# Loading order of batches 1 and 2 in an eight-batch attention and MLP kernel: the rest of k and v ahead of the main part, v ahead of the memsets, batch 2's k right behind w_out

## The chip, the core and the metric

The kernel runs on one core of one Trainium2 chip. That core has a matrix engine (PE), a vector engine (DVE), an activation engine (ACT), a general engine (POOL) and a sync engine (SP), and sixteen DMA engines that move data between the main memory and the on-chip memory. The metric is the device time of one execution in microseconds. Before the change it was 302.56 us, the median of three runs (302.47 to 302.97).

## What is computed

Attention over pooled keys and values, for 8 batches of 8 heads, 576 rows and 64 columns, and then a two-layer MLP over the 4608 resulting rows. Cut to what matters:

```python
k_p = k.reshape(B, H, 72, 8, D).mean(axis=3)      # eight rows pooled into one: 72 keys
v_p = v.reshape(B, H, 72, 8, D).mean(axis=3)
attn = softmax(q @ k_p.T / sqrt(D))
x = (attn @ v_p), as 4608 rows of 512
h = x @ w_in                                      # 512 x 2048
out = gelu_tanh(h) @ w_out                        # 2048 x 512
```

The 4608 rows are treated in nine groups of 512 (g = 0 to 8). A batch has 576 rows, so group g needs rows of batches g - 1 and g alone.

## The kernel before

The program is a software pipeline. While PE does the MLP of group g, the attention of batch g + 1 (called `nb`) is woven between the matrix products, and the inputs of batch g + 2 are loaded. The order on each engine is the order of the program text (`manual_schedule`), so an instruction that has to wait holds up all that stands behind it on its engine.

The pooled sums of k and v are made on DVE by three halving additions. A batch has 8 x 72 = 576 pooled rows of k, and the on-chip memory has 128 partitions: 512 rows (four per partition) are the main part, and the 64 rows left over, together with 64 rows left over of v, are a fifth slot called the rest. One function loads both:

```python
    def load_k(b, engs):
        rows = k[b].rearrange("h (j l) d -> (h j) (l d)", l=8)
        main = rows[0:128 * KR].rearrange("(p r) c -> p r c", r=KR)      # KR = 4
        n = KR // len(engs)
        for i, eng in enumerate(engs):
            eng.dma_start(out=kts[b % 2][:, i * n:(i + 1) * n], in_=main[:, i * n:(i + 1) * n])   # L74
        engs[0].dma_start(out=kts[b % 2][64:128, KR], in_=rows[128 * KR:])                         # L75
        rows = v[b].rearrange("h (j l) d -> j h (l d)", l=8)
        engs[-1].dma_start(out=kts[b % 2][0:64, KR], in_=rows[64:])                                # L77
```

Batches 0 and 1 use it and transpose their pooled keys on PE. From batch 2 on, another loader (`load_k_dma`, L82 to L85, the same bytes in another layout) is used, and q and the pooled keys are transposed by DMA (`trans_q_dma`, L264, and `trans_k_dma`, L185). The first loads behind batch 0's are issued by POOL in this order:

```python
    def load_rest():
        load_w_in(0, 2)
        load_w_in(2, 3)
        load_w_in(3, 4)
        load_k(1, [nc.gpsimd])
        load_q(1)
        for i in range(4):
            nc.gpsimd.dma_start(out=w_out_b[...], in_=w_out_v[:, i])       # L129
```

The three additions over the slots `c` (all five unless told otherwise), the small copy of the rest of v into the operand `vp` of the attention product, and the additions over half of batch 1's v:

```python
    def k_steps(b, c=slice(0, KR + 1)):
        t = kts[b % 2]
        return [lambda: add(t[:, c, 0:256], t[:, c, 0:256], t[:, c, 256:512]),     # add: L157
                lambda: add(t[:, c, 0:128], t[:, c, 0:128], t[:, c, 128:256]),
                lambda: add(kps[b % 2][:, c], t[:, c, 0:64], t[:, c, 64:128])]

    def v_moves(b):                                                                # L190
        (nc.scalar if b == 1 else nc.sync).dma_start(out=vps[b % 2][64:Sp, :, 0], in_=kps[b % 2][0:64, KR])

    def v_half(b, i):            # two of the four heads of each partition half
        t = vts[b % 2][:, 2 * i:2 * i + 2]
        ... two additions over t, then two more that write into vps[b % 2]         # all L157
```

At the end of batch 0's attention DVE clears buffers, and the load of batch 1's v follows one of these memsets (the SP queue waits for the one-column memset of L503, which stands there to set the moment of the load):

```python
    for t in kps:
        nc.vector.memset(t[:, KR + 1], 0.0)
    nc.vector.memset(kTs[1][0], 0.0)             # L498
    nc.vector.memset(kTs[1][1], 0.0)             # L499
    nc.vector.memset(vps[0], 8.0)                # L500

    for i in range(2):
        nc.vector.memset(vts[1][:, 2 * i, 0:1], 0.0)      # L503
    load_v(1, [nc.sync], 2)                               # four DMAs, L93
    nc.vector.memset(vps[1], 8.0)                # L505
    nc.gpsimd.memset(kz, 0.0)                    # L506
```

The loads for a later batch, called for batch 2 after the first half of group 0. The `gate` copies make POOL wait until something else has landed:

```python
        def load_next():
            if nb >= KX:                                                   # KX = 2
                nc.gpsimd.tensor_copy(out=gate, in_=eT[64:65, H - 1, 1, 0:2])
            if nb < KX:
                load_q(g + 2)                                              # L99
                trans_q_dma(g + 2)                                         # L264, issued by SP
                nc.gpsimd.tensor_copy(out=gate, in_=qTs[g + 2][0:1, 1, TP - 1, 0:2])   # L523
            if g + 2 >= KX:
                load_k_dma(g + 2)
            else:
                load_k(g + 2, [nc.gpsimd])
            load_v(g + 2, [nc.gpsimd])
            if nb >= KX:
                load_q(g + 2)
```

Group g has two halves. In the first, PE makes sixteen tiles of h (L406, four products each), ACT puts each through the gelu (L412), and side work is put behind the gelu with number `fo`:

```python
            kk = k_steps(nb) if nb < KX else k_steps_dma(nb)
            tk = [lambda: trans_k(nb, 4)]
            ...
            kk.append(lambda: v_moves(nb))
            ...
            else:           # g == 0
                tq = [...trans_q(nb, ...)...]
                plan = {0: kk[:-1], 11: kk[-1:], 13: tk, 14: tq[:1], 15: tq[1:3]}
```

In the second half PE makes the output (L415, 64 products, counted by m) with the attention of batch nb woven in. For group 0:

```python
                at(4, v_half, 1, 0)
                at(18, v_half, 1, 1)
            pos = (6, 14, 21, 27, 34, 41, 48, 55, 61)
            for i in range(len(ORDER) + 1):
                at(pos[i], qk, nb, *ORDER[i], 2)              # scores, L276
                a = (nb, *ORDER[i - 1], 4 + 2 * ((i - 1) % 2))
                at(pos[i], av, *a)                            # product with vp, L296
                at(pos[i], expo, nb, *ORDER[i], 2)            # ACT, L283
                at(pos[i], norm, *a)                          # ACT, L338, L339, L341
                at(min(pos[i] + 9, ...), mult, *a)            # DVE, L349: empties the banks that av filled
```

`av` alternates between two pairs of PSUM banks, so each `av` needs the `mult` of the one two places earlier to be done. DVE also empties the output banks: L650 (half sums kept for later), L421 and L424.

Of the kernel before, what the change touches and what calls it, by code (L numbers as in the profile page):

```python
# [18 lines left out]
def kernel(  # L19
# [9 lines left out]
    nc = tc.nc  # L29
# [13 lines left out]
    KR = 4  # L43
# [23 lines left out]
    KX = 2  # L67

    def load_k(b, engs):
        rows = k[b].rearrange("h (j l) d -> (h j) (l d)", l=8)  # L70
        main = rows[0:128 * KR].rearrange("(p r) c -> p r c", r=KR)
        n = KR // len(engs)
        for i, eng in enumerate(engs):
            eng.dma_start(out=kts[b % 2][:, i * n:(i + 1) * n], in_=main[:, i * n:(i + 1) * n])  # L74
        engs[0].dma_start(out=kts[b % 2][64:128, KR], in_=rows[128 * KR:])  # L75
        rows = v[b].rearrange("h (j l) d -> j h (l d)", l=8)
        engs[-1].dma_start(out=kts[b % 2][0:64, KR], in_=rows[64:])  # L77

    def load_k_dma(b):
        rows = k[b].rearrange("h (j l) d -> j h (l d)", l=8)  # L80
        for i in range(2):
            nc.gpsimd.dma_start(out=kts[b % 2][64 * i:64 * i + 64, 0:KR], in_=rows[0:64, 4 * i:4 * i + 4])  # L82
        nc.gpsimd.dma_start(out=kts[b % 2][64:128, KR], in_=rows[64:])
        rows = v[b].rearrange("h (j l) d -> j h (l d)", l=8)
        nc.gpsimd.dma_start(out=kts[b % 2][0:64, KR], in_=rows[64:])  # L85

    def load_v(b, engs, parts=1):

        rows = v[b].rearrange("h (j l) d -> j h (l d)", l=8)
        n = 4 // parts  # L90
        for r in range(0, 4, n):
            for i in range(2):
                engs[i % len(engs)].dma_start(out=vts[b % 2][64 * i:64 * i + 64, r:r + n],  # L93
                                              in_=rows[0:64, 4 * i + r:4 * i + r + n])

    def load_q(b, i0=0, i1=2):
        if b not in qs:
            qs[b] = qp.tile([128, 2, T * D], BF16, name="qb")
        nc.gpsimd.dma_start(  # L99
            out=qs[b][:, i0:i1],  # L100
            in_=q[b].rearrange("(i h) (p t) d -> (h p) i (t d)", i=2, t=T)[:, i0:i1])
# [7 lines left out]


    load_k(0, [nc.sync, nc.scalar])
    load_v(0, [nc.sync, nc.scalar])
    load_q(0, 0, 1)
    load_q(0, 1, 2)
# [2 lines left out]
    def load_w_in(k0, k1):  # L117
        nc.gpsimd.dma_start(out=w_in_b[k0 // 2][:, k0 % 2:k0 % 2 + k1 - k0], in_=w_in_v[:, k0:k1])
# [3 lines left out]
    def load_rest():  # L122
        load_w_in(0, 2)
        load_w_in(2, 3)
        load_w_in(3, 4)
        load_k(1, [nc.gpsimd])
        load_q(1)
        for i in range(4):
            nc.gpsimd.dma_start(out=w_out_b[:, 4 * i:4 * i + 4, :].rearrange("p j d -> p (j d)"), in_=w_out_v[:, i])  # L129
# [4 lines left out]
    kTs = [[consts.tile([128, H, Sp], BF16, name=f"kT{i}{e}") for e in range(2)] for i in range(2)]  # L134
# [6 lines left out]
    vps = [consts.tile([Sp, H, 2, D], BF16, name=f"vp{i}") for i in range(2)]  # L141
# [14 lines left out]
    def add(o, a, b):  # L156
        nc.vector.tensor_tensor(out=o, in0=a, in1=b, op=ALU.add)  # L157

    def k_steps(b, c=slice(0, KR + 1)):


        t = kts[b % 2]
        return [lambda: add(t[:, c, 0:256], t[:, c, 0:256], t[:, c, 256:512]),
                lambda: add(t[:, c, 0:128], t[:, c, 0:128], t[:, c, 128:256]),
                lambda: add(kps[b % 2][:, c], t[:, c, 0:64], t[:, c, 64:128])]

    def k_steps_dma(b):
        t = kts[b % 2]
        k0, k1 = (kz[:, :, e, e * D:e * D + D] for e in range(2))

        def third(o, p0, c):
            p = slice(p0, p0 + 64)
            return lambda: add(o, t[p, c, 0:64], t[p, c, 64:128])

        return [lambda: add(t[:, :, 0:256], t[:, :, 0:256], t[:, :, 256:512]),
                lambda: add(t[:, :, 0:128], t[:, :, 0:128], t[:, :, 128:256]),
                third(k0[:, 0:4], 0, slice(0, KR)), third(k0[:, 4:H], 64, slice(0, KR)),
                third(k0[:, H], 64, KR), lambda: nc.vector.tensor_copy(out=k1, in_=k0),
                lambda: trans_k_dma(b), third(kps[b % 2][0:64, KR], 0, KR)]
# [3 lines left out]
    def trans_k_dma(b):  # L183
        kxs[b] = bp.tile([128, 2 * H + 2, 64], BF16, name="kx", bufs=1)
        nc.sync.dma_start_transpose(out=kxs[b], in_=kz.rearrange("p h e c -> p (h e c)"))  # L185

    def v_moves(b):


        (nc.scalar if b == 1 else nc.sync).dma_start(out=vps[b % 2][64:Sp, :, 0], in_=kps[b % 2][0:64, KR])  # L190
# [10 lines left out]
    def v_steps(b):  # L201
        t = vts[b % 2]
        w = (vps[b % 2] if b else vz)[:, :, 0]

        def main():
            for i in range(2):
                p = slice(64 * i, 64 * i + 64)
                add(w[0:64, 4 * i:4 * i + 4], t[p, :, 0:64], t[p, :, 64:128])

        return [lambda: add(t[:, :, 0:256], t[:, :, 0:256], t[:, :, 256:512]),  # L210
                lambda: add(t[:, :, 0:128], t[:, :, 0:128], t[:, :, 128:256]), main]
# [25 lines left out]
    def trans_k(b, bank):  # L237
        trans_k_mm(b, bank)
        for e in range(2):
            trans_k_copy(b, e, bank)  # L240
# [17 lines left out]
    def trans_q(b, i, t0, n, bank, eng):  # L258
        trans_q_mm(b, i, t0, n, bank)
        trans_q_copy(b, i, t0, n, bank, eng)  # L260

    def trans_q_dma(b):
        qTs[b] = bp.tile([128, 2, TP, 128], BF16, name="qT")
        nc.sync.dma_start_transpose(out=qTs[b].rearrange("p i t c -> p (i t) c"),  # L264
                                    in_=qs[b].rearrange("p i c -> p (i c)"))
# [185 lines left out]

    nc.gpsimd.tensor_copy(out=gate[0:1], in_=kps[0][0:1, 0, 0:2])
    load_rest()
    scores(0, 0, 2)
    scores(0, 1, 0)
# [39 lines left out]
    mult0(1, 2, 2)  # L495
    for t in kps:
        nc.vector.memset(t[:, KR + 1], 0.0)
    nc.vector.memset(kTs[1][0], 0.0)  # L498
    nc.vector.memset(kTs[1][1], 0.0)  # L499
    nc.vector.memset(vps[0], 8.0)  # L500

    for i in range(2):
        nc.vector.memset(vts[1][:, 2 * i, 0:1], 0.0)  # L503
    load_v(1, [nc.sync], 2)
    nc.vector.memset(vps[1], 8.0)  # L505
    nc.gpsimd.memset(kz, 0.0)  # L506

    for fo, ko in [(fo, ko) for fo in range(6) for ko in range(2)]:
# [3 lines left out]
    for g in range(NG):  # L512
        nb = g + 1 if g + 1 < B else None
        act_set(GELU_SET)

        def load_next():

            if nb >= KX:
                nc.gpsimd.tensor_copy(out=gate, in_=eT[64:65, H - 1, 1, 0:2])  # L519
            if nb < KX:  # L520
                load_q(g + 2)
                trans_q_dma(g + 2)
                nc.gpsimd.tensor_copy(out=gate, in_=qTs[g + 2][0:1, 1, TP - 1, 0:2])  # L523
            if g + 2 >= KX:
                load_k_dma(g + 2)
            else:
                load_k(g + 2, [nc.gpsimd])
            load_v(g + 2, [nc.gpsimd])
            if nb >= KX:
                load_q(g + 2)  # L530

        if 0 < g and nb is not None and nb < KX:
            load_next()
# [1 line left out]

        side = {fo: [] for fo in range(FO)}
        if nb is not None:
            kk = k_steps(nb) if nb < KX else k_steps_dma(nb)
            tk = [lambda: trans_k(nb, 4)]
            if nb > KX:  # L540
                kk.append(lambda: trans_q_dma(nb))
            kk.append(lambda: v_moves(nb))
            vv = v_steps(nb)
            if nb >= KX:
                plan = {0: kk, 7: vv[:1], 8: vv[1:]}
            elif g:
                plan = {2: kk[:1], 3: kk[1:], 7: vv[:1], 8: vv[1:], 9: tk}
            else:
                tq = [lambda a=a, i=i: trans_q(nb, *a, QB[i], nc.vector) for i, a in enumerate(QG)]
                plan = {0: kk[:-1], 11: kk[-1:], 13: tk, 14: tq[:1], 15: tq[1:3]}  # L550
            for fo, what in plan.items():
                side[fo] += what

# [30 lines left out]
        if g == 0:  # L584
            load_next()
# [9 lines left out]
        if nb is not None and nb >= KX:  # L595
# [17 lines left out]
            if g + 2 < B:  # L613
                at(3, load_next)
# [41 lines left out]
    for c0, c1, bank in ((0, 384, o_bank(g, 3)), (384, DM, 4)):  # L656
# [5 lines left out]
        b, col = divmod(N - 128, S)  # L662
        t = col % CH // 32
        rows = out[b * S:(b + 1) * S].rearrange("(p t e) d -> e p t d", t=TP, e=2)
# [31 lines left out]
```

## Time and profile before

| what | value |
|---|---|
| time, median of 3 | 302.56 us |
| span of the profiled execution | 300.4 us |
| DVE, ACT, POOL busy | 152.7, 216.9, 38.2 us |
| bytes moved by DMA | 43.11 MB, 144 GB/s on average |
| start of group 0's matrix products | 20.0 us |
| group 0, second half | 34.9 to 54.65 us |
| group 1 | 54.65 to 85.89 us |
| groups 2 and 3, each | 31.08 us |

The views of the trace used here are the page of the whole run, the timeline of one engine (start, duration, line, operation, and in brackets how long the engine stood idle before and which event ended that), the table by stretches of time, the list of waits, and the chain of waits, which follows the work that ended last back to what released it. A line such as L157 is a line of the kernel before. A name such as `vp<-kp` says that `vp` is written from `kp`. In a line of POOLq, SPq or ACTq the duration is that of issuing a DMA and not that of the transfer. The trace also lists every DMA packet with its queue, size and start.

### The profile page before, as it was taken

How to read it: one execution, taken by the hardware profiler on the slowest of the kernel's cores; microseconds unless marked ns; L12 is line 12 of the kernel's file. 1: busy time of each engine (PE TensorE's matmuls, PEld its weight loads, DVE VectorE, ACT ScalarE, POOL GpSimd, SP SyncE). 2: the span in 40 equal slices, each digit the busy share in tenths (PEclk: the TensorE clock that was granted, in tenths of full speed). 3: DMA queues.
4: the chain of work that ended last, by engine and by line, in shares of the span. 5: the costliest groups of instructions: out<-in, count | busy, mean ns of one | idle time of the engine just before them, and what ended most of it. 6: DMA issues, size and time to landing. Idle time of an engine off the chain costs nothing.

```text
span 300.4 us, 4381 instructions
## 1 busy us (share of the span) xinstructions
PE 292.6 (97%) x1525; PEld 150.9 (50%) x1525; DVE 152.7 (51%) x308; ACT 216.9 (72%) x408; POOL 38.2 (13%) x69
## 2 busy tenths in 40 slices
PE   8799989999999999999999999999999999999995
PEld 3565545554555455545554555455545555445443
DVE  4785776475576257815690659155924630111112
ACT  1697677879888898789878988798879887206500
POOL 2614001300600060005000410033000000000000
PEclk9999999999999999999999999999999999999999
DMA  7999986871898169835994399729961210121022
GB/s 223 260 239 275 247 185 130 234 196 21 181 266 172 37 160 254 178 69 122 249 201 88 90 254 211 106 49 245 245 119 38 69 41 0 36 71 36 0 62 80
DMA packets 38806, 43.11 MB, mean 144 GB/s; under 512 B 25536, under 2 KB 26176, under 8 KB 38656
## 3 DMA queue, kind: packets, MB, share of 16 engines
q0 software_dynamic: 8016, 24.39, 35.7%
q1 hardware_dynamic: 30064, 17.06, 25.1%
q10 hardware_dynamic: 704, 1.38, 1.3%
q8 instruction: 12, 0.20, 0.3%
q14 instruction: 10, 0.08, 0.1%
HBM read 36.70 MB, written 9.44 MB: 154 GB/s over the span
## 4 chain that ended last, share of the span: by engine, by line
PE 78%; DMA 12%; DVE 4%; ACT 3%; issue 1%; SPq 1%; POOL 0%; DVEq 0%; POOLq 0%
PE PS L415 36%; PE PS L406 32%; DMA vt<-in_v_dram 5%; PE PS L331 4%; DMA kt<-in_v_dram 3%; PE PS L320 2%; DMA kt<-in_k_dram 2%; DMA qT<-qb 2%; DVE kt L157 1%; DMA kx<-kz 1%; PE PS L658 1%; ACT e L283 1%; PE PS L305 1%; ACT rc L365 1%; PE PS L276 1%
## 5 line engine op out<-in xcount | busy, mean ns | idle before, releaser
L415 PE MATMUL PS<-w_out_b,gT 128*128 128x512 bf16 x560 | 136.9, 379 | 0.0
L406 PE MATMUL PS<-xT,w_in_b 128*128 128x512 bf16 x576 | 126.2, 379 | 0.0
L412 ACT ACTIVATE gT<-PS 128x512 bf16<-128x512 f32 x144 | 79.3, 608 | 44.2 <-PE PS L406 44.1
L406 PEld LDWEIGHTS <-w_in_b 128*128 128x128 bf16 x576 | 65.1, 113 | 58.7
L415 PEld LDWEIGHTS <-gT 128*128 128x128 bf16 x560 | 53.9, 97 | 51.5 <-issue 2.1
L349 DVE TENSOR_TENSOR xT<-PS,rc 64x288 bf16<-64x288 f32 x112 | 51.0, 455 | 19.8 <-ACT rc L341 17.2
L421 DVE COPY osb<-PS 128x512 f32<-128x512 f32 x33 | 22.8, 692 | 50.0 <-PE PS L415 44.4
L326 ACT ACTIVATE eT<-PS 64x576 bf16<-64x576 f32 x48 | 30.7, 640 | 0.6
L313 DVE COPY eT<-er 8x576 bf16<-8x576 bf16 x24 | 7.3, 303 | 38.9 <-ACT er L311 38.3
L338 ACT ACTIVATE ld<-PS 64x288 f32<-64x288 f32 x56 | 22.6, 403 | 5.6 <-PE PS L331 5.1
L341 ACT ACTIVATE rc<-ld 128x288 f32<-128x288 f32 x56 | 24.9, 444 | 1.8
L157 DVE TENSOR_TENSOR kt<-kt 128x1280 f32<-128x1280 f32 (+5 forms) x18 | 18.9, 1048 | 11.5 <-DMA kt<-in_v_dram 7.5
L383 ACT ACT_TABLE_LOAD x17 | 21.8, 1283 | 3.6 <-issue 3.3
L339 ACT ACTIVATE ld<-PS 64x288 f32<-64x288 f32 x56 | 22.6, 403 | 1.4
L331 PE MATMUL PS<-eT,vp 72*128 72x288 bf16 x96 | 19.7, 285 | 0.0
L519 POOL COPY gate<-eT 1x2 bf16<-1x2 bf16 x5 | 0.9, 177 | 125.0 <-DMA eT<-er 125.0
L157 DVE TENSOR_TENSOR vt<-vt 128x512 f32<-128x512 f32 (+2 forms) x18 | 15.6, 865 | 1.4 <-DMA vt<-in_v_dram 1.0
L331 PEld LDWEIGHTS <-vp 72*128 72x128 bf16 x96 | 9.5, 98 | 11.3
L283 ACT ACTIVATE e<-PS 72x576 bf16<-72x576 f32 x16 | 9.9, 644 | 4.5 <-PE PS L276 4.4
L435 PE MATMUL PS<-idle 128*128 128x512 bf16 x31 | 8.9, 433 | 1.2 <-DVE idle L146 1.2
L320 PE MATMUL PS<-qT,kx 128*128 128x288 bf16 x48 | 9.8, 286 | 0.0
L559 DVE COPY kt<-gT 128x512 bf16<-128x512 bf16 x4 | 3.0, 744 | 11.6 <-ACT gT L412 11.6
(68 smaller groups left out, 131.6 us busy)
## 6 DMA issues: line engine op xcount, KB each, us to landing
out_dram<-osb SPq DMA_DIRECT2D x141, 64.0 KB
kt<-in_k_dram POOLq DMA_DIRECT2D x12, 512.0 KB, 6.9
vt<-in_v_dram POOLq DMA_DIRECT2D x12, 512.0 KB, 10.7
qb<-in_q_dram POOLq DMA_DIRECT2D x7, 576.0 KB, 14.8
w_out_b<-in_moe_w_out_dram POOLq DMA_DIRECT2D x4, 512.0 KB, 19.7
w_in_b<-in_moe_w_in_dram POOLq DMA_DIRECT2D x1, 1024.0 KB, 9.7
w_in_b<-in_moe_w_in_dram POOLq DMA_DIRECT2D x2, 512.0 KB, 12.4
kt<-in_k_dram POOLq DMA_DIRECT2D x1, 1024.0 KB, 16.4
```

Source lines behind the costliest of these rows:

```text
L157: nc.vector.tensor_tensor(out=o, in0=a, in1=b, op=ALU.add)
L326: nc.scalar.activation(out=eT[0:64, 2 * pr:2 * pr + 2, c, :], in_=PS[64 * c:64 * c + 64, 2:4, :CH], func=ACT.Exp, scale=1.0 / 64.0)
L331: nc.tensor.matmul(out=PS[:, bank + x, :CH], lhsT=window(vps[b % 2], 2 * pr + x), rhs=eT[:, 2 * pr + x, c, :], start=True, stop=True)
L338: nc.scalar.activation(out=ld[0:64], in_=PS[64:128, bank, :CH], func=ACT.Ln)
L339: nc.scalar.activation(out=ld[64:128], in_=PS[0:64, bank + 1, :CH], func=ACT.Ln)
L341: nc.scalar.activation(out=rc, in_=ld, func=ACT.Exp, scale=-1.0)
L349: nc.vector.tensor_tensor(out=xT[rows, pr, col:col + CH], in0=PS[rows, bank + x, :CH], in1=rc[rows], op=ALU.mult)
L383: nc.scalar.preload_act_table_set(name)
L406: nc.tensor.matmul(out=PS[:, h_bank(g, fo), :], lhsT=w, rhs=xT[:, ko, r0:r0 + GROUP], start=(ko == 0), stop=(ko == KO - 1))
L412: nc.scalar.activation(out=gTs[g][:, fo, :], in_=PS[:, h_bank(g, fo), :], func=ACT.Gelu_apprx_tanh)
L415: nc.tensor.matmul(out=PS[:, bank], lhsT=gTs[g][:, fo, r * 128:(r + 1) * 128], rhs=w_out_b[:, fo], start=(fo == first), stop=(fo == last))
L421: nc.vector.tensor_copy(out=osb, in_=PS[:, bank])
```

## The change

The change moves loads and sums of the two batches that follow batch 0. The loading of the rest becomes a function of its own (`load_rem`); for batch 1 it is issued ahead of the main part, its sums are made first, and the copy of the rest of v into `vp` is issued behind gelu 7 in place of gelu 11. The load of batch 1's v is released ahead of four memsets, three of which stood in front of it. Batch 2's k is loaded right behind its q, and so right behind w_out on POOL's queue, and no longer waits until q has been transposed; its v still does. It is meant to have these operands ready earlier. Nothing of the arithmetic changes.

```diff
+    def load_rem(b, engs):
+        rows = k[b].rearrange("h (j l) d -> (h j) (l d)", l=8)
         engs[0].dma_start(out=kts[b % 2][64:128, KR], in_=rows[128 * KR:])
         ...
     load_k(0, [nc.sync, nc.scalar])
+    load_rem(0, [nc.sync, nc.scalar])
     ...
         load_w_in(3, 4)
+        load_rem(1, [nc.gpsimd])
         load_k(1, [nc.gpsimd])
     ...
-    nc.vector.memset(kTs[1][0], 0.0)
-    nc.vector.memset(kTs[1][1], 0.0)
-    nc.vector.memset(vps[0], 8.0)
     for i in range(2):
         nc.vector.memset(vts[1][:, 2 * i, 0:1], 0.0)
     load_v(1, [nc.sync], 2)
-    nc.vector.memset(vps[1], 8.0)
+    nc.vector.memset(kTs[1][0], 0.0)
+    nc.vector.memset(kTs[1][1], 0.0)
+    for w in vps:
+        nc.vector.memset(w, 8.0)
     nc.gpsimd.memset(kz, 0.0)
     ...
                 load_q(g + 2)
+            load_k_dma(g + 2)
+            if nb < KX:
                 trans_q_dma(g + 2)
                 nc.gpsimd.tensor_copy(out=gate, in_=qTs[g + 2][0:1, 1, TP - 1, 0:2])
-            if g + 2 >= KX:
-                load_k_dma(g + 2)
-            else:
-                load_k(g + 2, [nc.gpsimd])
             load_v(g + 2, [nc.gpsimd])
     ...
-            kk = k_steps(nb) if nb < KX else k_steps_dma(nb)
+            kk = k_steps(nb, slice(KR, KR + 1)) if nb < KX else k_steps_dma(nb)
     ...
-                plan = {0: kk[:-1], 11: kk[-1:], 13: tk, 14: tq[:1], 15: tq[1:3]}
+                plan = {0: kk[:-1] + k_steps(nb, slice(0, KR)), 7: kk[-1:], 13: tk, 14: tq[:1], 15: tq[1:3]}
```

## The prediction

> **What bounds the kernel now.** I read the page first, then the table by stretches, then PE's and DVE's timelines in the stretch that stood out, and last the chain of waits across group 1.
>
> ```profile
> PE 292.6 (97%) x1525; PEld 150.9 (50%) x1525; DVE 152.7 (51%) x308; ACT 216.9 (72%) x408; POOL 38.2 (13%) x69
> ```
>
> PE is busy 97% of the span, so only its losses can be won. But a busy PE isn't a PE at its rate, so I look for the rate: the chain of waits has 64 products of L406 in 13.81 us, 216 ns each. With that I check the stretches (columns: length, PE busy, then other engines):
>
> ```profile
> 34.90:54.65 19.75, 18.72 (x103) 9.75 (x101) 13.69 (x30) 15.64 (x32) 3.31 (x7) 1.00 0.77 168
> 54.65:85.89 31.24, 31.15 (x162) 15.87 (x160) 17.45 (x35) 26.30 (x52) 5.15 (x9) 1.00 0.70 170
> 85.89:116.97 31.08, 31.08 (x162) 15.91 (x161) 17.66 (x35) 26.41 (x52) 4.61 (x8) 1.00 0.71 160
> ```
>
> Groups 2 and 3 take 31.08 us each with no idle PE: nothing to win there. Group 1 takes 31.24, 0.16 more. The second half of group 0 has to do 64 products at 0.216 (13.8 us), 16 score and 16 value products at about 0.12 (3.9) and the last 10 or so transposes at about 0.06 (0.6), 18.3 in all, and takes 19.75. So some 1.4 to 1.7 us are lost between 34.9 and 54.65, and 0.16 in group 1. The first 20 us, batch 0's own attention, are a long chain of their own which the change leaves alone. PE's timeline shows where the losses sit:
>
> ```profile
> 39.00 0.40 PE L296 MATMUL PS<-e,vp 72*128 72x288 bf16 x2 [0.20 <-DMA vp<-kp]
> 43.36 0.28 PE L296 MATMUL PS<-e,vp 72*128 72x288 bf16 x1 [0.41 <-DVE xT L349]
> 43.85 0.28 PE L296 MATMUL PS<-e,vp 72*128 72x288 bf16 x1 [0.21 <-DVE xT L349]
> 48.33 0.28 PE L296 MATMUL PS<-e,vp 72*128 72x288 bf16 x1 [0.21 <-DVE xT L349]
> ```
>
> The first waits for the copy of the rest of v; the others for DVE to empty the banks. The brackets understate the loss, as matmuls overlap, so I take starts. At 38.39 two score products start, which end their turn at 38.63; the value products could start then and start at 39.00: 0.37 lost. At 42.54 the same happens: PE is due at 42.78 and goes on to L415 at 43.98, 1.20 later for 0.25 of work: 0.95 lost. At 47.84 it is 0.61 for 0.25: 0.36 lost. Why DVE is late at 43 is in its timeline:
>
> ```profile
> 39.87 0.69 DVE L650 COPY osb<-PS 128x512 f32<-128x512 f32 x1 [1.02 <-PE PS L415]
> 41.04 1.15 DVE L157 TENSOR_TENSOR vt<-vt 128x512 f32<-128x512 f32 x2 [0.48 <-DMA vt<-in_v_dram]
> 42.23 0.60 DVE L157 TENSOR_TENSOR vp<-vt 64x128 bf16<-64x128 f32 x2
> 42.86 1.92 DVE L349 TENSOR_TENSOR xT<-PS,rc 64x288 bf16<-64x288 f32 x4
> ```
>
> DVE stands 0.48 us until the second half of batch 1's v has landed, then sums it (1.79 us to 42.83), and only then empties the banks for which PE waits. Group 1's 0.16 is in the chain of waits:
>
> ```profile
> 53.38 7.81 DMA kt<-in_v_dram
> 61.27 1.50 DVE kt L157
> ...
> 65.16 3.95 DMA kx<-kz
> 69.15 0.44 PE PS L305 x7
> ```
>
> Batch 2's k lands at 61.2, is summed, transposed by DMA, and the first products that use it start at 69.15, though PE was due at 68.90.
>
> **What the Trainium skill says, and the trace.** "Perfetto Trace Analysis", Identifying the Most-Contended Engine: busy time of matmuls doesn't tell how near PE is to its limit, since they are pipelined. The trace agrees: L415 has a mean of 379 ns, yet one leaves every 216 ns. "DMA: Bandwidth & Descriptors", Queues, rings and completion order: each DMA engine takes its queues in turn, packet by packet. The trace agrees: from 27.1 to 39.6 us the 512 packets of batch 1's v (2048 bytes, SP's queue, 95 ns each) and the packets of w_out and q (POOL's queue, 4096 bytes mostly, 322 ns) go at about 40 per us each. Same page, Anatomy of one DMA: most of a small DMA's fixed time is the receipt after the last byte. The last packet of v starts at 39.58 and DVE goes on at 41.04, 1.46 later; that agrees. Same page, Rules for kernel authors: a DMA transpose beside ordinary DMAs needs no care for its result. What it costs in time isn't stated, and no run so far shows it, since the transpose of batch 2's q had the engines to itself (2304 packets of 256 bytes between 46.69 and 49.60).
>
> **The change, part by part.**
>
> *v ahead of memsets.* SP's four issues started at 23.70, right behind DVE's memsets L498, L499 (0.30 us each) and L500 (0.91, with gaps 1.63 from 21.99). Without these they start at about 22.1, 1.6 earlier. DMA engines are full from the start to about 44 us, but v takes turns with whatever POOL's queue holds, so its 12.5 us shift whole: last packet near 38.0, landed near 39.4. What POOL's queue loses early (batch 1's q lands under 1 us later, used at 33.25; w_out's first quarter later by as much, used at 34.9) it gets back by the end of w_out. The same memsets are still done, by 24.8, ahead of the sums.
>
> *The rest first.* The rest is 256 KB: it should land near 24.3 (w_in landed at 23.5, by POOL's wait for it). Its sums (some 0.97 us, from batch 0's rest: 0.75 and 0.22) run from 24.8, while DVE waited until 27.95 anyway; the main sums then cost 2.38 in place of 2.84 and end where they did or 0.4 earlier, ahead of PE's transposes at 32.11. On the path: nothing. ACT issues the copy of the rest of v at 28.5 instead of 30.86, for 0.72 us of its queue. Gelus 8 to 11 slip by up to that; tile 12, due on PE at 30.39, needs gelu 8, then done at about 29.7. Hidden. The copy took 8.1 us between issue and 39.00, so it should be there near 36.6: the 0.37 at 39.00 is gone.
>
> *DVE's chain at 43.* With PE 0.37 earlier, L650 starts at 39.50 and ends at 40.19. If v has landed (39.4), the sums run from 40.22 to 42.02, the two multiplications end at 42.5 and 43.0, and PE, due at 42.41, goes on to L415 at about 43.15 instead of 43.98. So both waits together bring 0.83, of which 0.37 is in the first; half of the 0.95 stays, since the sums themselves are too long. The loss at 48 stays: there DVE follows PE (0.69 for L421 and 0.94 for two multiplications against some 1.55 of PE's work).
>
> *Batch 2's k.* It is queued behind q, whose last packet starts at 44.7, and lands at about 50 instead of 61. DVE sums it from 56, when its multiplications end, so the transposed k is there at about 64 and the wait at 68.90 is gone: 0.16. It collides with the transpose of q from 46.7 to about 49: 320 or so large packets in turn with 256-byte ones. I expect that transpose to end 2 us later (53 for 50.95), the gate of v with it, and the stores behind it on SP's queue; v is needed at 65.76 and has 1 MB to move, less than the 2.3 MB that k and v moved from 53 to 65.7 before. Hidden.
>
> Sum: 0.83 + 0.16 = 0.99 us, all on PE's path. 302.56 - 0.99 = 301.57, say 301.6.
>
> **The rivals.** (1) v doesn't land earlier: if it is slowed by the main part of k that now stands beside it, DVE still starts at 41.04. The wait at 39 merely moves to 43, and only group 1's 0.16 is left: 302.4. For it speaks that the DMA share is near 1 in all of this time; against it that turns are taken per packet. (2) The transpose of q is hurt far more than 2 us by k's packets. Then SP's stores, behind it in the queue, and the transpose of the pooled k behind those, are late, and v's gate with them: PE would wait in group 1 for 1 to 3 us, 303 to 305. For it speaks that the kernel before kept those transfers apart with a gate; against it, 8 us of room. (3) More is won: if v lands early and PE's later turns line up better, the losses at 43 and 48 shrink further: at most 1.7 + 0.16, 300.7.
>
> **Range and chances.** A gain of 0.8 to 1.1 is the likeliest (60%), rival 1 has about 15%, rival 2 10%, rival 3 15%. So 300.9 to 302.6 should hold 8 in 10. 2% is 6 us, and no loss of that size is within reach: 0.97 for within 2%.
>
> **What would show it right or wrong.** Right: no wait for `vp<-kp` at 39; DVE without a wait for v ahead of the sums of L157 near 40.2; group 0's second half about 0.8 shorter; group 1 at 31.08; the first 20 us unchanged. Wrong: DVE still waiting for v there; `kx<-kz` landing after 68; PE waiting for w_out near 35, or for ACT near 30. Beyond those, a change of more than 0.2 us in any group past 1 would be something that I haven't seen.

## The result, and the profile after

The changed kernel takes 301.38 us, the median of six runs (301.13 to 301.47), against 302.54 for the kernel before (six runs). The ratio is 0.996, with a 95% interval of 0.9947 to 0.9973: some 1.2 us less (0.8 to 1.6). The change adds a function and moves statements, so most lines of the kernel after that are named here are three to seven higher: L157 is L162, L296 is L301, L349 is L354, L305 is L310, L406 is L411, L415 is L420, L523 is L530.

PE's line on the page of the kernel after:

```profile
PE 293.4 (98%) x1525; PEld 151.4 (51%) x1525; DVE 153.1 (51%) x311; ACT 216.8 (72%) x408; POOL 38.0 (13%) x69
```

The stretches, from where their first products start (group 0's second half, groups 1 and 2):

```profile
34.92:53.87 18.95, 18.53 (x103) 9.82 (x101) 13.70 (x30) 15.63 (x32) 0.47 (x1) 1.00 1.10 212
53.87:84.95 31.08, 31.08 (x161) 15.89 (x160) 17.43 (x35) 26.17 (x52) 6.01 (x11) 1.00 0.64 145
84.95:116.03 31.08, 31.08 (x161) 15.88 (x160) 17.66 (x35) 26.39 (x52) 4.60 (x8) 1.00 0.72 158
```

Group 0's second half is 18.95 us long (19.75 before) and group 1 is 31.08 (31.24): 0.80 and 0.16 less, 0.96 together. The start, 34.92, has hardly moved (34.90). PE's timeline at the places where it waited before:

```profile
38.65 0.41 PE L301 MATMUL PS<-e,vp 72*128 72x288 bf16 x2
...
42.58 0.28 PE L301 MATMUL PS<-e,vp 72*128 72x288 bf16 x1
43.07 0.28 PE L301 MATMUL PS<-e,vp 72*128 72x288 bf16 x1 [0.21 <-DVE xT L354]
...
47.55 0.28 PE L301 MATMUL PS<-e,vp 72*128 72x288 bf16 x1 [0.21 <-DVE xT L354]
...
68.21 0.44 PE L310 MATMUL PS<-qT,kx 128*16 128x288 bf16 x8
```

At 38.65 the wait for the copy of the rest of v is gone. At 43 some is left: two products due at 42.44 let L420 go on at 43.19, 0.50 late. The loss at 47 is as it was. At 68.21 the transposed k of batch 2 is there in time. DVE's timeline tells the same from its side:

```profile
39.53 0.69 DVE L653 COPY osb<-PS 128x512 f32<-128x512 f32 x1 [0.67 <-PE PS L420]
40.26 1.15 DVE L162 TENSOR_TENSOR vt<-vt 128x512 f32<-128x512 f32 x2
41.44 0.60 DVE L162 TENSOR_TENSOR vp<-vt 64x128 bf16<-64x128 f32 x2
42.08 1.92 DVE L354 TENSOR_TENSOR xT<-PS,rc 64x288 bf16<-64x288 f32 x4
...
56.17 2.35 DVE L162 TENSOR_TENSOR kt<-kt 128x1280 f32<-128x1280 f32 x2
```

No wait for v ahead of 40.26, nor for batch 2's k ahead of 56.17. What the early k costs is at the transpose of batch 2's q, first as SP's issue of it, then as the gate that waits for it on POOL (the issue took 2.81 us before, and the gate came at 50.95):

```profile
46.42 5.59 SPq L269 DMA_TRANSPOSE qT<-qb  x1
```
```profile
54.16 0.17 POOL L530 COPY gate<-qT 1x2 bf16<-1x2 bf16 x1 [18.77 <-DMA qT<-qb]
```

It ends some 3 us later than before, and PE doesn't wait for it. The trace has one loss that the kernel before didn't have, in group 3:

```profile
130.63 0.44 PE L310 MATMUL PS<-qT,kx 128*16 128x288 bf16 x8 [0.19 <-DMA qT<-qb]
```

That group takes 31.34 us, 0.26 more than its neighbours. No trace of the other thirteen shows this wait, so it is one late landing and no effect that the change is known to have.

### The profile page after: what moved, and what is told of

Its sections match the earlier page's. It is cut to its first block, busy times and chain, and to the rows that moved or that the text cites. A ratio compares the mean times of both kernels' runs of the same rounds, so it can differ in the third digit from the quotient of the medians.

```text
span 299.7 us, 4384 instructions
## 1 busy us (share of the span) xinstructions
PE 293.4 (98%) x1525; PEld 151.4 (51%) x1525; DVE 153.1 (51%) x311; ACT 216.8 (72%) x408; POOL 38.0 (13%) x69
## 4 chain that ended last, share of the span: by engine, by line
PE 86%; DMA 7%; DVE 2%; issue 1%; POOL 1%; ACT 1%; POOLq 0%; SPq 0%; DVEq 0%
PE PS L411 37%; PE PS L420 36%; DMA qb<-in_q_dram 5%; PE PS L336 3%; PE PS L440 3%; PE PS L325 2%; DMA qT<-qb 2%; PE PS L661 1%; PE PS L281 1%; PE PS L310 1%; PE PS L377 1%; DMA eT<-er 1%; ACT e L288 1%; DVE xT L354 1%; PE PS L301 1%
## 5 line engine op out<-in xcount | busy, mean ns | idle before, releaser
L420 PE MATMUL PS<-w_out_b,gT 128*128 128x512 bf16 x560 | 136.9, 379 | 0.0
L411 PE MATMUL PS<-xT,w_in_b 128*128 128x512 bf16 x576 | 126.2, 379 | 0.0
L411 PEld LDWEIGHTS <-w_in_b 128*128 128x128 bf16 x576 | 65.1, 113 | 58.8
L420 PEld LDWEIGHTS <-gT 128*128 128x128 bf16 x560 | 53.9, 97 | 51.4 <-issue 2.1
L354 DVE TENSOR_TENSOR xT<-PS,rc 64x288 bf16<-64x288 f32 x112 | 51.0, 455 | 19.7 <-ACT rc L346 17.1
L162 DVE TENSOR_TENSOR kt<-kt 128x1280 f32<-128x1280 f32 (+5 forms) x20 | 19.2, 959 | 5.6 <-DMA kt<-in_k_dram 4.9
L162 DVE TENSOR_TENSOR vt<-vt 128x512 f32<-128x512 f32 (+2 forms) x18 | 15.6, 865 | 2.7 <-DMA vt<-in_v_dram 2.3
L440 PE MATMUL PS<-idle 128*128 128x512 bf16 x31 | 10.0, 474 | 1.2 <-DVE idle L151 1.2
L562 DVE COPY kt<-gT 128x512 bf16<-128x512 bf16 x4 | 3.0, 744 | 11.6 <-ACT gT L417 11.6
## 6 DMA issues: line engine op xcount, KB each, us to landing
w_in_b<-in_moe_w_in_dram POOLq DMA_DIRECT2D x2, 512.0 KB, 12.3
```

The source lines that it names most:

```text
L354: nc.vector.tensor_tensor(out=xT[rows, pr, col:col + CH], in0=PS[rows, bank + x, :CH], in1=rc[rows], op=ALU.mult)
L411: nc.tensor.matmul(out=PS[:, h_bank(g, fo), :], lhsT=w, rhs=xT[:, ko, r0:r0 + GROUP], start=(ko == 0), stop=(ko == KO - 1))
L420: nc.tensor.matmul(out=PS[:, bank], lhsT=gTs[g][:, fo, r * 128:(r + 1) * 128], rhs=w_out_b[:, fo], start=(fo == first), stop=(fo == last))
```

## The experiments

One trace is one execution, and landings differ from one to the next. So the table has the times as medians of many runs, and beside them what each single trace says of groups 0 and 1: the time from the first product of group 0 to the first of group 2. The ratio is to the kernel before on the same chip. The medians of the kernel before are 302.50 for the four runs from "rest first alone" to "all but k early", 302.68 for the four from "all but rest first" to "two moves on DVE", and 302.49 for the others but the first, so medians from different groups can be 0.2 apart for that reason alone.

For every run the span from its first instruction to its last is known too; the time is some 2 us longer. The column of gains gives both parts, as means against the kernel before on the same chip (a minus is a loss).

| run | median us (runs) | ratio, 95% interval | mean gain in the span, outside it | its trace, groups 0 and 1 |
|---|---|---|---|---|
| before, first trace | 302.54 (6) | | | 65.87 |
| before again | 302.50 (12) | 0.9999 (0.9991 to 1.0008) | 0.05, -0.04 | 65.97 |
| rest first alone | 302.12 (13) | 0.9989 (0.9981 to 0.9998) | 0.25, 0.15 | 65.81 |
| v early alone | 302.13 (13) | 0.9993 (0.9984 to 1.0002) | 0.34, -0.06 | 66.50 |
| k early alone | 302.41 (13) | 0.9996 (0.9988 to 1.0005) | 0.19, -0.05 | 65.88 |
| all but k early | 301.76 (15) | 0.9972 (0.9963 to 0.9981) | 0.54, 0.18 | 65.93 |
| all but rest first | 302.12 (11) | 0.9981 (0.9972 to 0.9990) | 0.59, 0.06 | 65.18 |
| all but v early | 301.89 (8) | 0.9972 (0.9962 to 0.9982) | 0.67, 0.23 | 65.56 |
| whole change again | 301.46 (5) | 0.9961 (0.9948 to 0.9975) | 0.97, 0.28 | 64.93 (first trace 64.91) |
| two moves on DVE | 300.99 (5) | 0.9944 (0.9932 to 0.9956) | 1.61, 0.14 | 64.39 |
| v's addition moved | 300.94 (5) | 0.9946 (0.9932 to 0.9960) | 1.39, 0.19 | 64.41 |
| and later products | 301.75 (10) | 0.9975 (0.9966 to 0.9984) | 0.91, -0.20 | 64.88 |
| and q ahead of v | 301.74 (9) | 0.9974 (0.9964 to 0.9983) | 0.94, -0.16 | 64.89 |

The time outside the span differs between the kernels: its mean is 1.96, 2.06 and 1.97 us for the kernel before on the three chips in this order, 2.00 to 2.02 for the three other kernels without the first part (the rest first), and 1.76 to 1.91 for those with it, but for the last two rows, which have 2.17 and 2.13. Why is open. What the traces explain is the gain in the span.

**The parts alone.** The first:

```diff
+        load_rem(1, [nc.gpsimd])
         load_k(1, [nc.gpsimd])
         ...
-            kk = k_steps(nb) if nb < KX else k_steps_dma(nb)
+            kk = k_steps(nb, slice(KR, KR + 1)) if nb < KX else k_steps_dma(nb)
         ...
-                plan = {0: kk[:-1], 11: kk[-1:], 13: tk, ...}
+                plan = {0: kk[:-1] + k_steps(nb, slice(0, KR)), 7: kk[-1:], 13: tk, ...}
```

> Of the three parts of the change, only the rest of batch 1's k and v loaded and summed first, and its copy into vp behind gelu 7. My theory: the wait for the copy at 39 on PE is gone (0.37), but batch 1's v still lands near 41.0, so DVE starts its sums then and PE waits that much longer near 43: gain 0.0 (at most 0.1), 302.5. Rival theory, that each wait counts for itself: 0.37 less, 302.2.

Measured: 0.38 less by the medians (by the interval 0.06 to 0.57), which is the rival's number. The trace says otherwise. DVE, then PE:

```profile
41.50 1.15 DVE L162 TENSOR_TENSOR vt<-vt 128x512 f32<-128x512 f32 x2 [0.93 <-DMA vt<-in_v_dram]
```
```profile
43.82 0.28 PE L301 MATMUL PS<-e,vp 72*128 72x288 bf16 x1 [0.87 <-DVE xT L354]
```

The wait for the copy at 39 is gone and the wait at 43 is longer by about as much; groups 0 and 1 gain 0.06 (0.16 against the second trace of the kernel before, below). The trace supports my mechanism, the median rather the rival's size. Much of the difference is outside the span, where this kernel gains 0.15; the 0.25 that its span gains is uncertain by some 0.2.

The second part:

```diff
-    nc.vector.memset(kTs[1][0], 0.0)
-    nc.vector.memset(kTs[1][1], 0.0)
-    nc.vector.memset(vps[0], 8.0)
     for i in range(2):
         nc.vector.memset(vts[1][:, 2 * i, 0:1], 0.0)
     load_v(1, [nc.sync], 2)
-    nc.vector.memset(vps[1], 8.0)
+    ... (the four memsets)
```

> Only batch 1's v let go ahead of the memsets. My theory: v lands near 38.6 to 39, DVE no longer waits for it (0.48 less at 43), but the copy of the rest, issued at 30.86 as before, still makes PE wait near 39 for up to 0.37: gain 0.45, 302.1. If v, being out of the way sooner, lets the copy through in time as well, the gain is 0.8, 301.75, and the copy's earlier issue was worth nothing by itself. The rival of a loss: v beside the main part of k delays k's sums past 32.1 and PE's transposes wait.

Measured: 0.37 less by the medians (the interval reaches from 0.5 less to none). In the trace DVE no longer waits for v, and PE waits for the copy all the longer:

```profile
39.69 0.41 PE L296 MATMUL PS<-e,vp 72*128 72x288 bf16 x2 [0.69 <-DMA vp<-kp]
```

So v's early end doesn't let the copy through: its last packet goes at 38.72, no sooner than before (38.24). This execution, one of the longer ones (302.78), lost more than it gained (66.50): PE waited for w_out, so that group 0's second half began at 35.09, 0.35 later behind the first product than in any other trace here, and for `kx`, so that group 1 took 31.46. The prediction had named a wait for w_out near 35 as a sign of being wrong; among the fourteen traces it stands in this one alone.

The third part:

```diff
                 load_q(g + 2)
+            load_k_dma(g + 2)
+            if nb < KX:
                 trans_q_dma(g + 2)
                 nc.gpsimd.tensor_copy(out=gate, ...)
-            if g + 2 >= KX:
-                load_k_dma(g + 2)
-            ...
```

> Only batch 2's k loaded right behind its q. My theory: group 1 takes 31.08 in place of 31.24 and nothing else moves: gain 0.16, 302.4, though the transpose of q takes 3 us longer. Rival: the collision delays what stands behind it and PE waits in group 1: slower by 0.5 or more.

Measured: 0.09 less by the medians, within the noise, and the trace shows no wait for `kx` and none behind the transpose of q: group 1 takes 31.08. The rival of a harmful collision is out. That the part wins something is not shown by this run, as group 1 takes 31.08 in the second trace of the kernel before as well.

**One part left out.** The first two parts without the third:

> The whole change without batch 2's k. My theory: group 0's second half 0.8 shorter, group 1 stays at 31.24: gain 0.8, 301.75. Together with the run of k alone this is the whole change's 1.0 to 1.15. Rival: if k's early load also helps elsewhere (the rest of the 1.16 measured), this run gains 0.8 and that one alone more than 0.16.

Measured: 0.74 less. But the runs fall in two lots: nine between 301.43 and 301.77, six between 302.04 and 302.35; the trace is of the slowest, and shows what cost it most:

```profile
69.27 0.44 PE L310 MATMUL PS<-qT,kx 128*16 128x288 bf16 x8 [0.96 <-DMA kx<-kz]
```

Group 0 gave PE 0.8 us, and group 1, which my theory had at 31.24, took it back with 32.11: batch 2's k lands at 61.25, as in the first trace of the kernel before, and the transposed k is there at 69.2, whenever PE comes. The wait was short there because PE was late itself. In the whole change PE starts that product at 68.21. The nine shorter executions, with about the time of the whole change, have no trace; that k landed sooner in them would fit, as its landing does vary (60.14 in the second trace of the kernel before), but is not shown.

The second and third parts without the first, and the first and third without the second:

```diff
 # all but the rest first: the kernel after, with
-        load_rem(1, [nc.gpsimd])
-        load_k(1, [nc.gpsimd])
+        load_k(1, [nc.gpsimd])          # main part, then rest, as before
         ...                             # and kk over all five slots
-                plan = {0: kk[:-1] + k_steps(nb, slice(0, KR)), 7: kk[-1:], 13: tk, ...}
+                plan = {0: kk[:-1], 11: kk[-1:], 13: tk, ...}
 # all but v early: the kernel after, with
-    load_v(1, [nc.sync], 2)             # ahead of the memsets
+    load_v(1, [nc.sync], 2)             # behind three of them, as before
```

> The change without its first part: v early and batch 2's k early, but the rest of k and v loaded and summed as before, its copy behind gelu 11. My theory now, that the parts cover for each other because what PE waits for are landings at fixed times: the copy is what PE waits for near 39 (0.3 to 0.7), so most of the gain of the other two is lost: about 302.1 where the whole change is 301.4. Rival, each part counts for itself (measured alone 0.38, 0.37 and 0.09 less): 301.4 and 0.38, 301.8.

> The change without its second part: v let go behind the memsets as before. My theory now: no wait for the copy at 39, but DVE waits 0.6 to 0.9 for v near 40.5 and PE as much near 43; left of the gain is 0.1 to 0.3: 302.3. Rival, each part for itself: 301.4 and 0.37, 301.8.

> The changed kernel once more, as the measure for the other three runs beside it: 301.4 by every theory, with no wait for the copy at 39 nor for v at 40, and 0.5 left at 43 and 0.36 at 47.

Measured: without the first part 302.12, which is the number of my theory; without the second 301.89, which is nearer to the rival's 301.8 than to my 302.3; the whole 301.46. The 302.12 owes something to luck: in its trace the products at 39 start at 39.19, 0.29 late, groups 0 and 1 are only 0.27 longer than in the whole change, and 0.2 of the 0.66 is outside the span.

In the span, the first part is worth 0.38 on top of the other two, the second 0.30, the third 0.43; alone they were worth 0.25, 0.34 and 0.19, together 0.78 of the whole's 0.97. Each of these numbers is uncertain by 0.2 to 0.3, so the times don't show that a part is worth more in company. That one wait feeds the next is seen in the traces: at 39 and 43 in that of the first part alone, at 69 in that of all but k early. In the trace without the second part DVE waits as expected, and groups 0 and 1 keep 0.31 of the gain:

```profile
41.10 1.15 DVE L162 TENSOR_TENSOR vt<-vt 128x512 f32<-128x512 f32 x2 [0.69 <-DMA vt<-in_v_dram]
```

**A second trace of the kernel before**, with no edit:

> The kernel before once more, for a second trace of it: 302.5. My theory, that the parts only seemed worth too much or too little because landings vary from one execution to the next: the waits at 39, 43 and 69 are there again, each off by 0.1 to 0.5 from those of the first trace, and group 0's start is off by up to 0.4. Rival, that one trace stands for all: each wait within 0.05 of the first trace.

Measured: 302.50. The two waits of group 0 in this execution, PE then DVE then PE:

```profile
38.73 0.41 PE L296 MATMUL PS<-e,vp 72*128 72x288 bf16 x2
```
```profile
41.28 1.15 DVE L157 TENSOR_TENSOR vt<-vt 128x512 f32<-128x512 f32 x2 [0.98 <-DMA vt<-in_v_dram]
```
```profile
43.60 0.28 PE L296 MATMUL PS<-e,vp 72*128 72x288 bf16 x1 [0.92 <-DVE xT L349]
```

Here the products at 39 start 0.12 late, PE is due at 42.52, earlier than in the first trace (42.78), and is let go on later, at 44.22 instead of 43.98. The wait at 39 was worth nothing without the one behind it: v's landing sets the end of both. At 69 this execution loses nothing, as PE comes later and batch 2's k landed at 60.14, 1.13 sooner than in the first trace. So my theory holds but for its sizes, and the rival is out: one trace doesn't stand for all. The losses at 39, 43 and 69 together (0.37 + 0.95 + 0.16 = 1.48 in the first, 0.12 + 1.45 + 0.00 = 1.57 in the second, with the excess of group 1 over 31.08 taken for the third) vary less than each.

**What is left.** Two moves on DVE in group 0, then the first of them alone:

```diff
+                at(13, v_first, 1, 1)       # v's first addition, ahead of the second half-sum copy
                 at(18, v_half, 1, 1)        # the other three
 # in the first run only, the multiplication of place 3 ahead of the store of m = 35:
-                    at(min(pos[i] + 9, ...), mult, *a)
+                    at(35 if i == 3 else min(pos[i] + 9, ...), mult, *a)
```

> The changed kernel with two instructions of DVE moved in group 0: the first addition over the second half of batch 1's v ahead of the second half-sum copy, where DVE stands 0.67, and the multiplication of place 3 at m = 35, ahead of the store. My theory, that what is left at 43 and 47 is the order of DVE's work and no transfer: 0.5 and 0.36 less, 300.5, with group 0's second half at 18.1. Rival: v's second half is not there yet at 38.9, the addition waits in front of the copy and PE waits for the copy's bank at 40.7: gain 0.36 at most, 301.0 or worse.

> The changed kernel with the first addition over the second half of v moved ahead of the second half-sum copy, and nothing else. Theory: the 0.5 left at 43 is gone and the 0.36 at 47 stays: 0.5 below the changed kernel, 300.95, so that in the run with both moves the move of the multiplication won nothing, as it only moved the wait to the store's bank. Rival, that the two moves had a share each: 301.2.

Measured: 300.99 and 300.94, against 301.46 for the whole change; groups 0 and 1 take 64.39 and 64.41 in the traces, against 64.91 and 64.93. The addition alone brings all of it, 0.5, and neither of the two kernels is shown to be faster than the other. The number of the first is its rival's 301.0, but not for the rival's reason: the addition starts at 39.29 without a wait for v. The next two lines are DVE's and PE's with the addition moved alone (here L296 is L306 and L349 is L359):

```profile
39.04 0.69 DVE L162 TENSOR_TENSOR vt<-vt 128x512 f32<-128x512 f32 x1
```
```profile
42.59 0.41 PE L306 MATMUL PS<-e,vp 72*128 72x288 bf16 x2
```

The addition fills the 0.67 in which DVE waited for PE, and the two products at 42.59 follow each other without a gap. The moved multiplication brought nothing: it had to wait for ACT until 45.12, and the store behind it then held PE at 46.84 in its place.

Then the products of the sixth place two later, and on top of it q ahead of v from batch 3 on:

```diff
-            pos = (6, 14, 21, 27, 34, 41, 48, 55, 61)
+            pos = (6, 14, 21, 27, 34, 43, 48, 55, 61)
 # second run also:
-            load_v(g + 2, [nc.gpsimd])
             if nb >= KX:
                 load_q(g + 2)
+            load_v(g + 2, [nc.gpsimd])
```

> As the run before it, and the sixth place of the attention's products at m = 43 in place of 41, so that PE has two products of w_out to do while DVE stores and multiplies. Theory: the 0.36 at 47 goes as well and nothing takes its place: 300.6. Rival: ACT's chain behind that place is late by the same 0.4 and PE waits at the next one: 300.95.

> As the run before it, and from batch 3 on q loaded ahead of v. In the trace of the changed kernel PE waited once, in group 3, 0.26 for q's transpose. Theory: q then lands 3 to 5 us sooner, DVE waits up to 3 us for v where it is idle anyhow, no wait for q is left in any execution: 0 to 0.2 below the run before it, 300.5. Rival: v's additions come late for the products that use them: slower by 0.3 or more.

Measured: 301.75, a miss, 0.81 worse than without the later products. Of this, 0.48 is in the span (0.47 in the trace of groups 0 and 1) and the rest outside it. The loss at 47 is gone, but a larger one stands at the place after the next:

```profile
51.56 0.28 PE L306 MATMUL PS<-e,vp 72*128 72x288 bf16 x1 [0.25 <-DVE xT L359]
```

The multiplication of the moved place comes nine products after it, so it went from m = 50 to m = 52, behind the store of m = 51 on DVE, which waits for PE. PE, due at 51.15, goes on 0.78 late, against the 0.36 saved. It isn't ACT's chain, as the rival had it. With q ahead of v the time is the same, 301.74: DVE's waits for v are up to 2.8 us and cost nothing, as expected, but SP's transpose of q follows that of k by 1.42 us in group 3 of both runs, so there was no late q to be cured in either trace. Whether the order would spare a wait such as the one in group 3 stays open.

## Why the prediction was right, and where its working was not

The predicted time was 301.6 and the measured one 301.38, inside the range of 300.9 to 302.6; the predicted gain of 0.99 compares with 0.96 in the traces of groups 0 and 1, 0.97 in the spans of the later runs and 1.16 in the medians.

- *v ahead of memsets.* SP's issue moved from 23.70 to 22.04 and DVE waited no more at 40.26, as predicted. All packet times in the prediction were read 0.66 us too early, against a wrong zero. On the right one DVE went on 0.81 us after v's last packet had started, not 1.46. That packet started at 40.23 before and at 37.70 after: 2.5 earlier and not 1.6, as the packets of v no longer took 12.5 us but 11.6. They took 12.3 to 12.9 in the traces with only one of the first two parts, so the two help each other here; for DVE, ready at 40.26, 1.6 would have been enough.
- *The rest first.* Its sums ran from 24.85 to 25.87, the copy was issued at 27.21 (predicted 28.5), ACT's delay was hidden, and PE took the products at 38.65 without a wait. That this wins nothing unless v is early too, as the term of 0.83 for both together has it, is what the trace of the first part alone shows.
- *DVE's chain at 43.* L653 at 39.53, the sums from 40.26, L420 at 43.19: predicted 39.50, 40.22 and 43.15. Half of the loss, 0.50, stayed. The reason given was the length of DVE's sums; the more exact one is their place behind the wait for PE, as moving one addition ahead of it removed the loss with the work as long as before.
- *Batch 2's k.* The term of 0.16 was mis-sized. It was read off the wait at 69 as it stood in the first trace (where 0.25 late was one estimate and group 1's 0.16 the better one), but a wait for a landing that doesn't depend on PE grows by what PE gains ahead of it: to 0.96 in the trace of the run without the third part. What this part is worth in the whole change is known only roughly: 0.30 by the medians of 301.76 and 301.46, 0.43 by the spans. The total came out right because the change has all three parts: with the third in it, group 1 gives back nothing of the 0.83 from group 0. The path was also longer than thought: the last packet of the transposed k ended at 66.11, where the prediction had it there at about 64, so that 2 and not 4 us were to spare before 68.2.
- *The collision.* The gate behind the transpose of q ran at 54.16, where 53 was expected, and the delay was hidden.
- *Rivals 1 and 2* are refuted by the two traces of the changed kernel: no wait for v, none in group 1. *Rival 3* is in part what the moved addition did; the change itself didn't, as 0.50 was left at 43 and 0.36 at 47.

The 0.2 between 0.96 and 1.16 is not PE's: the second measurement of the change gains 0.97 in the span, which is the prediction's sum, and 0.28 outside it, which the prediction didn't have. The time outside the span is shorter in every kernel with the first part, but for the two in which the sixth place is moved, and what causes this is open. Open too is whether the first part alone gains 0.06 in the span, as its trace says, or 0.25, as the mean of its runs does.

## What to carry to other kernels

When several waits in a row are for transfers whose landing doesn't depend on the waiting engine, the wait that a trace shows at each is what the waits ahead of it have left over: removing one feeds the next, so judge the parts together, and each by leaving it out as well as by doing it alone. A single trace can mislead by as much as such a wait is long, so take two before sizing one. Compare a change of time with the change of the span: what lies outside no wait on PE explains. Release loads ahead of fixed work such as memsets, and let an engine fill a gap ahead of an ordered wait with the first piece of what comes behind it. Before moving an instruction, look where its followers fall in the order of the other engines: two products of delay put a multiplication behind a store, where PE lost 0.78 to save 0.36.

## What the runs showed of the hardware

A DMA transpose that shares the DMA engines with a bulk load is slowed but works on: its 2304 packets of 256 bytes took 2.9 us alone (21 ns each) and 4.6 us beside batch 2's k (27 ns each; 3.9 to 5.6 us in the nine traces that have both), and SP spent 5.59 us instead of 2.81 on issuing it. The 8 KB copy of the rest was no quicker when v alone ended 1.6 us sooner (38.63 for 40.23): from issue to last packet it took 7.59 us instead of 7.38. Issued 3.65 us earlier (27.21 instead of 30.86) in the kernel after, its last packet went 4.2 us earlier (34.08 instead of 38.24).
